# A gated linear attention and feed-forward kernel: TensorE's pads of NOPs placed anew, and the first four total decays turned two heads at a time

## The chip, the cores and the metric

One core of a Trainium2 chip runs the whole program. The metric is the device time of one execution in microseconds (us); the time before is a median of three runs, 522.33 us (521.56 to 523.01).

A core has several engines that run side by side, each with a queue of its own: TensorE (PE; loading the stationary operand is shown apart as PEld), VectorE (DVE), ScalarE (ACT), GpSimd (POOL), and SyncE (SP), which issues the transfers (DMA) here. They wait for each other by semaphores. Each engine has a sequencer that takes the instructions in order and hands them to the engine.

## The reference

Four batches, eight heads, 768 steps, head size 48. In the first half a state of 48 by 48 per head decays by `alpha` and takes in a product of `k` and `v` at each step; the second half is a feed-forward layer with a squared ReLU over 3072 tokens.

```
for t in range(S):
    state = alpha[:, :, t, :, None] * state + np.einsum('bhd,bhe->bhde', k[:, :, t], v[:, :, t])
    y[:, :, t] = np.einsum('bhd,bhde->bhe', q[:, :, t], state)
x = np.ascontiguousarray(y.transpose(0, 2, 1, 3)).reshape(B * S, H * D)
h = np.maximum(x @ w_in, 0.0)
out = (h * h) @ w_out
```

The shapes are `w_in` 384 by 2048 and `w_out` 2048 by 384. Both weights come as 64-bit floats, which the kernel turns into FP32 itself.

## The kernel before, in words

**Tiling.** The 768 steps are cut into six chunks of 128, so there are 24 blocks of 128 tokens (four batches times six chunks), in groups of four blocks (`GB = 4`). For a block, `ln` takes logarithms of alpha, `cs` sums them along the chunk with one product on TensorE, `eb` and `ei` make the running decay `b` and its inverse with exponentials on ScalarE, `mq` and `mk` scale q by `b` and k by the inverse on VectorE, `qT` and `kT` (in later groups `turn`) transpose them on TensorE, `sc`, `kv`, `am` and `us` make scores, state sums, masked scores and sums, `ya` and `yb` give the block's output y, `ev` copies it away, and `st` gives the next state, for which it needs the decay over the whole chunk.

**The total decay.** It is the last row of `b`, needed as a column per head. In the first four blocks TensorE turns it: `lt` (line 345) multiplies, for each of the eight heads, the head's 48 columns of `b` by the last column of the identity matrix; one moving column, a stationary operand of 128 by 48, and the result goes to partitions 0 or 64, by the head's parity. Two copies on ScalarE (line 357) bring it to SBUF. In later blocks a round trip through DRAM does this (`bl`, `br`).

**Stages and order.** The first 33 us are a start in which the first four blocks are prepared; the order of its steps is the list `first` in `AT`, written out by hand, with some products into a bank that nobody reads (`fill`) where TensorE would sit idle. Then six groups follow: each has an input layer and an output layer of the feed-forward part, into which the attention steps of the next group are woven by events with a time in units of work (`weave`). Group 0 works on plain FP32 operands (lines 926 and 816), the later ones on split FP32R operands in three passes (line 733 for the input layer, line 816 for the output layer).

**How products become instructions.** Each pass of a product is a weight load and a matmul. A product of FP32 operands takes two passes, a transpose or an FP32R product one; with this rule the program's products make 5350 matmuls, the number on the page.

**Pads.** Three times the kernel calls `align` (line 1009), at the `turn` of blocks 4, 14 and 16 (`places` in `AT`). `addr_align(256, offset=place)` puts NOPs into TensorE's program until the next instruction stands at place `place` in a block of 256 instructions. The trace has 159 such NOPs: 59, 78 and 22 of them. Counted through the program in this way, the last pads come out at exactly 78 and 22, and the 59 of the first say that 62 places lie ahead of the first instruction counted. So the place of every instruction in its block of 256 is known.

**Waiting.** Most of TensorE's instructions carry their wait with them; where one needs two, a semaphore instruction of the sequencer stands ahead of it, and the sequencer stops there.

Of the kernel before, what the change touches and what calls it, by code (L numbers as in the profile page):

```python
# [12 lines left out]
AF = mybir.ActivationFunctionType  # L13
ALU = mybir.AluOpType
# [1 line left out]


GB = 4
AT = {'v_by': (2.5, 3.5, 5.0), 'before': 2.2, 'places': ((4, 203), (14, 178), (16, 188)), 'evs': 0.65, 'lead': 4, 'post': 3, 'w_first': (45.25, 42.0, 55.95), 'wstep': 1.6, 'w_in_at': 2.5, 'w_in_by': 3.4, 'room1': 22, 'room': 25, 's0': 4, 'ahead': 6, 'late': 2, 'xs': 0.2, 'g0': ((1.5, 4, False, True, 28.25), (20.25, 6, True, True), (28.75, 8, True, False)), 'sc0': (2.35, 2.35, 2.35), 'g1': ((5.5, 8, False, 15.5), (15.5, 10, True), (34.5, 12, True)), 'g': ((1.7, 6, True), (15.5, 8, True)), 'g1x': 50.0, 'gx': 48.25, 'g0x': 55.25, 'k0': 2, 'h0': 16, 'k1': 4, 'h1': 3, 'h1by': 2, 'evs0': 0.3, 'tp': 'ADMD', 'tp1': 'ADAD', 'split': 8, 'o0': (44.75, 47.25), 'o1': (), 'o2': (21.75, 27.5, 31.75, 35.0, 41.25, 41.75), 'str1': 22.0, 'ga': 9.5, 'gb': 13.0, 'cv0': 1.5, 'first': 'ln0 warm0 cs0 load0v load2a ei0 load1v eb0 mk0 ln1 fill1 fill1 kT0 cs1 kc0 eb1 mq0 qT0 mq1 ei1 qc0 fill1 mk1 fill1 lt0 sc0 lt1 kT1 kv0 qT1 am0 ln2 weights2 us0 load2q kc1 qc1 cs2 sc1 fill1 am1 load2k ei2 load3a eb2 load4a fill1 kv1 st0 first0 us1 fill1 middle0 ln3 mq2 load3k ya0 qT2 yb0 mk2 fill1 qc2 kT2 cs3 kc2 load3q load2v weights5 sc2 eb3 load3v fill1 sga0 weights3 sgb0 fill1 ei3 ev0 mq3 mk3 am2 fill1 qT3 kT3 sgc0 first1 kc3 qc3 middle1 kv2 weights4 ha0 sc3 us2 kv3 sga1 ha1 am3 us3 sgb1 load4k ya2 load4q load4v first2 yb2 sgc1 middle2 weights6 lt3 ev2 lt2 st2 ha3 ha2 sgb2 sga2 hb1 sgc2 hb0 hb2 weights1 st1 hb3 st3 weights0'}


RUN = {0: 128, 32: 32, 64: 64, 96: 32}
# [3 lines left out]
def kernel(  # L26
# [12 lines left out]
    nc = tc.nc  # L39
    B, H, S, D = q.shape  # L40
    C = 128
# [39 lines left out]
    def two_k(name, dt=FP32, shape=(GB * C,)):  # L81
        return two_pool.tile([128, *shape], dt, tag="two", name=name)
# [7 lines left out]
    def flat(t):  # L90
        return t.rearrange("a x y -> a (x y)")
# [3 lines left out]
    for x, n in (("q", 2), ("q", 3), ("k", 3)):  # L95
        t = lent[x, n] = two_k("qk_lent", shape=(H, 64))
        nc.gpsimd.memset(t[:, :, D:64], 0.0)

    def tile_of(x, n):
        return lent.get((x, n), tiles[x][n % len(tiles[x])])  # L100
# [127 lines left out]
    ident = consts.tile([128, 128], FP32, name="ident")  # L228
# [9 lines left out]
    for t in s_all + u_all:  # L238
        nc.gpsimd.memset(t, 0.0)
    last = consts.tile([128, 4, NP], FP32, name="last")  # L240
    nc.gpsimd.memset(last, 0.0)
    last_t = [last[:, i, :] for i in range(4)]
    dram = ctx.enter_context(tc.tile_pool(name="dram", bufs=1, space=bass.MemoryType.DRAM))
# [15 lines left out]
    blk = [{} for _ in range(NBLK)]  # L259
# [4 lines left out]
    def bank(n, name, shape=(NP, C)):  # L264

        return ps_att.tile([128, *shape], FP32, tag="att", name=name)
# [10 lines left out]

    SPLIT = AT["split"]

# [22 lines left out]
    def sums_of_logs(n):  # L302
        return blk[n]["cs"].rearrange("a p t -> a (p t)")[:, 0 : H * D]

    def eb(n):
        b = blk[n]["b"] = p2.tile([128, H * D], FP32, tag="b", name="b")
        nc.scalar.activation(out=b, in_=sums_of_logs(n), func=AF.Exp)

# [3 lines left out]

    def scaled(x, n, factor):
        t = tile_of(x, n)[:, :, 0:D]
        nc.vector.tensor_tensor(
            out=t, in0=t, in1=factor.rearrange("a (h d) -> a h d", h=H), op=ALU.mult
        )

    def mq(n):
        need(("q", n))  # L320
        scaled("q", n, blk[n]["b"])
        given.add(("qb", n))

    def mk(n):
        need(("k", n))
        scaled("k", n, blk[n].pop("inv"))
        given.add(("kb", n))
# [17 lines left out]
    def lt(n):  # L345

        ps = bank(n, "lastT")
        for p in range(NP):
            for e in range(2):
                nc.tensor.matmul(  # L350
                    out=ps[64 * e : 64 * e + D, 0, p : p + 1],
                    lhsT=blk[n]["b"][:, (2 * p + e) * D : (2 * p + e + 1) * D],
                    rhs=ident[:, C - 1 : C], start=True, stop=True, skip_group_check=True,
                )
        for e in range(2):
            rows = slice(64 * e, 64 * e + D)
            nc.scalar.copy(out=last_t[n % 4][rows, :], in_=ps[rows, 0, 0:NP])
        given.add(("last", n))
# [290 lines left out]
    here, todo, room = {}, [], [22]  # L649
# [28 lines left out]
    def diff_w(w, p):  # L678
# [5 lines left out]
        for x in "ld":  # L684
            t = made.pop((x, w, p))
            if w == "i" or p >= NW - AT["k0"] or (x == "l" and p >= NW - AT["k1"]):
                here[x, w, p] = t
        pump()

    def prepare(at, w, p):  # L690
        step = AT["wstep"]
        fs = (cast_w, rest_w, scale_w, diff_w)
        return [(at + i * step, f, (w, p)) for i, f in enumerate(fs)]
# [82 lines left out]
    def splits_of_x(at, g):  # L776
        return [(at + i * AT["xs"], f, (g, i % KM)) for i, f in enumerate((split_x,) * KM + (diff_x,) * KM)]

    def layer_in(g):
        units = []  # L780
        for n in range(NJ + 2):
            if n < NJ:
                units.append((1.05, in_x, (n,)))
            if 0 <= n - 2 < NJ:
                units.append((0.53, in_y, (n - 2,)))
            if 0 <= n - AT["post"] < NJ:
                units.append((0, in_post, (n - AT["post"],)))
            if AT["lead"] <= n < AT["lead"] + AHEAD and (g > 1 or AT["k1"] == NW):
                units += splits_of_h(0, n - AT["lead"])
        return units  # L790
# [168 lines left out]


    steps = {f.__name__: f for f in (ln, sp, cs, eb, ei, mq, mk, bl, br, lt, qT, qc, kT, kc, ev)}
    steps["sc"], steps["kv"], steps["am"] = scores, state_sums, masked
    steps["us"], steps["st"] = sums_copied, next_state
# [14 lines left out]
    first = AT["first"]  # L978
# [28 lines left out]
    places = dict(AT["places"])  # L1007
# [51 lines left out]
    def weave(units, events, at):  # L1059
        for cost, f, args in units:  # L1060
            while events and events[0][0] <= at:
                _, e, given = events.pop(0)
                e(*given)
            f(*args)
            at += cost
        for _, e, given in events:
            e(*given)
# [44 lines left out]
    base = [0]  # L1112
    cv0 = AT["cv0"]
    events = [(3.4 * i + cv0, next_weights, (3 + i,)) for i in range(-3, 2 * NW - 3) if ("mid", 3 + i) not in given]
# [11 lines left out]
    for g in range(1, NG):  # L1126
        base.append(begin + sum(u[0] for u in units))
        at0 = base[g]
        units.append((0, begun, (g,)))
        units += layer_in(g) + layer_out(g)  # L1130
        units.append((0, ended, (g,)))
        if g + 1 < NG:
            for t, n0, after, *other in AT["g1"] if g == 1 else AT["g"]:
                n0 = n0 if g == 1 else n0 + GB * g
                other = [None if x is None else at0 + x for x in other]
                events += attention(at0 + t, n0, after, 1, True, *other)
            events += [(at0 + t, f, x) for t, f, x in splits_of_x(AT["g1x" if g == 1 else "gx"], g + 1)]
        if g == 1:
            m = len(AT["w_first"])
            for p in range(m, NW):  # L1140
                events += prepare(at0 + AT["w_in_at"] + AT["w_in_by"] * (p - m), "i", p)
            for i, at in enumerate(AT["o1"] + AT["o2"]):
                events += prepare(at0 + at, "o", order[len(AT["o0"]) + i])
            n = min(AT["k0"], AT["k1"])
            events.append((at0, lambda: todo.extend(("l", "o", p) for p in range(NW - n, NW)), ()))
            events.append((at0 + AT["str1"], stream_out, (AT["k1"], "d")))
        events.append((at0 + 26, stream, (g + 1,)))
    weave(units, sorted(events, key=lambda x: x[0]), begin)


# [28 lines left out]
```

## Time and profile before

| what | before |
|---|---|
| median of 3 runs | 522.33 us |
| the profiled execution's own time | 521.93 us |
| its span, from first to last instruction | 520.1 us |
| granted TensorE clock, mean | 0.999 |
| TensorE busy | 511.3 us, 5350 matmuls |
| VectorE busy | 362.3 us |
| ScalarE busy | 315.6 us |
| HBM traffic over the span | 195 GB/s |
| TensorE busy of the first 33 us | 29.44 us |
| TensorE busy from 33 to 125 us | 92.00 us |
| TensorE busy from 219 to 226 us | 5.32 us of 7 |

The profiled execution's time is 1.83 us more than its span, and 0.40 us under the median of the runs. Times of single instructions below are counted from the start of the span. A line such as `9.74 0.53 PE L350 MATMUL lastT<-ident,b 128*48 128x1 f32 x16` says: from 9.74 us on, for 0.53 us, 16 matmuls of line 350 on TensorE, with a stationary operand of 128 by 48 and one moving column; in brackets at the end stands the idle time before it and what ended it. Matmuls are pipelined: the time from one start to the next, and not the duration, is what one costs. `PEldq` is the sequencer of TensorE's queue.

### The profile page before, as it was taken

How to read it: one execution, taken by the hardware profiler on the slowest of the kernel's cores; microseconds unless marked ns; L12 is line 12 of the kernel's file. 1: busy time of each engine (PE TensorE's matmuls, PEld its weight loads, DVE VectorE, ACT ScalarE, POOL GpSimd, SP SyncE). 2: the span in 40 equal slices, each digit the busy share in tenths (PEclk: the TensorE clock that was granted, in tenths of full speed). 3: DMA queues.
4: the chain of work that ended last, by engine and by line, in shares of the span. 5: the costliest groups of instructions: out<-in, count | busy, mean ns of one | idle time of the engine just before them, and what ended most of it. 6: DMA issues, size and time to landing. Idle time of an engine off the chain costs nothing.

```text
span 520.1 us, 13202 instructions
## 1 busy us (share of the span) xinstructions
PE 511.3 (98%) x5350; PEld 421.9 (81%) x5350; DVE 362.3 (70%) x629; ACT 315.6 (61%) x664; POOL 5.3 (1%) x29
## 2 busy tenths in 40 slices
PE   8999999999999999989999999999999999999997
PEld 6775446668887669968899988899988899988997
DVE  3987979999879579757596466696465485363861
ACT  5678893687999566466953266962266863164620
POOL 4000000000000000000000000000000000000000
PEclk9999999999999999999999999999999999999999
DMA  9999686417888496998885796955683534798201
GB/s 185 214 269 253 180 209 180 67 61 231 242 229 199 121 279 162 309 306 227 183 238 163 245 268 185 227 174 163 214 273 123 182 123 153 252 355 294 70 0 62
DMA packets 139324, 102.36 MB, mean 197 GB/s; under 512 B 109808, under 2 KB 112896, under 8 KB 139264
## 3 DMA queue, kind: packets, MB, share of 16 engines
q1 hardware_dynamic: 139264, 101.52, 68.5%
q8 instruction: 43, 0.70, 0.5%
q14 instruction: 17, 0.14, 0.1%
HBM read 84.17 MB, written 17.33 MB: 195 GB/s over the span
## 4 chain that ended last, share of the span: by engine, by line
PE 92%; DVE 3%; ACT 2%; DMA 1%; issue 1%; SPq 0%; DVEq 0%; POOLq 0%
PE o L816 40%; PE h L733 31%; PE h L926 8%; PE y L409 4%; PE sckv L429 2%; PE T L586 2%; PE sckv L457 2%; DMA a_in<-in_alpha_dram 1%; ACT x L624 1%; PE cs L296 1%; PE cs L299 1%; PE cs L300 1%; DVE x L624 0%; DVE osb L656 0%; DVE xl L656 0%
## 5 line engine op out<-in xcount | busy, mean ns | idle before, releaser
L733 PE MATMUL h<-xa,wb 128*128 128x512 f32 x240 | 69.2, 396 | 0.0
L733 PE MATMUL h<-xd,wd 128*128 128x512 f32 x240 | 66.9, 394 | 1.8 <-ACT ha L706 1.7
L733 PE MATMUL h<-xl,wl 128*128 128x512 f32 x240 | 68.2, 392 | 0.0
L750 ACT ACTIVATE h<-h 128x512 f32<-128x512 f32 x40 | 23.3, 582 | 57.5 <-PE h L733 57.3
L656 DVE TENSOR_TENSOR hid<-h,hid 128x512 f32<-128x512 f32 x40 | 27.5, 688 | 42.7 <-PE h L733 39.9
L624 ACT COPY x<-y 32x256 f32<-32x256 f32 (+2 forms) x132 | 47.1, 364 | 15.2 <-PE y L409 13.0
L816 PE MATMUL o<-wb,ha 128*128 128x384 f32 x160 | 54.2, 339 | 0.0
L733 PEld LDWEIGHTS h<-xd,wd 128*128 128x128 f32 x240 | 44.4, 188 | 11.6 <-ACT ha L706 2.1
L816 PE MATMUL o<-wd,hd 128*128 128x384 f32 x304 | 53.7, 335 | 0.0
L816 PE MATMUL o<-wl,hl 128*128 128x384 f32 x160 | 53.6, 335 | 0.0
L816 PE MATMUL o<-w_out,hid 128*128 128x384 f32 x160 | 53.5, 490 | 0.0
L733 PEld LDWEIGHTS h<-xl,wl 128*128 128x128 f32 x240 | 44.9, 188 | 10.5 <-ACT wl L675 0.6
L816 PEld LDWEIGHTS o<-wd,hd 128*128 128x128 f32 x304 | 52.8, 188 | 0.0
L733 PEld LDWEIGHTS h<-xa,wb 128*128 128x128 f32 x240 | 44.3, 188 | 9.5 <-ACT xa L706 0.3
L816 PE MATMUL o<-wb,hx 128*128 128x384 f32 x144 | 48.8, 339 | 0.0
L816 PE MATMUL o<-wl,hx 128*128 128x384 f32 x144 | 48.2, 335 | 0.0
L816 PEld LDWEIGHTS o<-w_out,hid 128*128 128x128 f32 x160 | 30.0, 190 | 19.6
L926 PE MATMUL h<-x,w_in 128*128 128x512 f32 (+1 forms) x120 | 42.8, 510 | 0.2 <-DVE w_in L206 0.2
L706 ACT ACTIVATE ha<-hid 128x512 fp32r<-128x512 f32 x40 | 25.5, 636 | 23.8 <-DVE hx L656 13.1
L748 ACT ACTIVATE hid<-h 128x512 f32<-128x512 f32 x40 | 24.2, 606 | 25.2 <-PE h L733 25.1
L926 PEld LDWEIGHTS h<-x,w_in 128*128 128x128 f32 x120 | 22.5, 190 | 17.2 <-issue 14.2
L656 DVE TENSOR_TENSOR hl<-hid,ha 128x512 fp32r<-128x512 f32 x40 | 27.5, 686 | 11.2 <-ACT ha L706 11.2
(115 smaller groups left out, 883.7 us busy)
## 6 DMA issues: line engine op xcount, KB each, us to landing
wd<-do SPq DMA_DIRECT2D x36, 384.0 KB
wl<-lo SPq DMA_DIRECT2D x34, 384.0 KB
wl<-li SPq DMA_DIRECT2D x32, 384.0 KB
wd<-di SPq DMA_DIRECT2D x32, 384.0 KB
raw<-in_moe_w_in_dram SPq DMA_DIRECT2D x8, 768.0 KB
raw<-in_moe_w_out_dram SPq DMA_DIRECT2D x8, 768.0 KB
v_in<-in_v_dram SPq DMA_DIRECT2D x24, 192.0 KB
out_dram<-osb SPq DMA_DIRECT2D x24, 192.0 KB
```

The source lines that it names most:

```text
L409: ins = nc.tensor.matmul(out=ys[e][64 * half : 64 * half + D + G * e, m % 2, p // 2, t], lhsT=lhsT, rhs=rhs, start=(half, e) not in seen, ...
L429: nc.tensor.matmul(out=ps[e][HALF[h], 0, p, :], lhsT=ks[rows, p, HALF[h]], rhs=qs[rows, p, HALF[h]], start=True, stop=True, skip_group_che ...
L457: nc.tensor.matmul(out=ps[h][64 * e : 64 * (e + 1), 1, p, G:64], lhsT=tile_of("k", n)[HALF[h], 2 * p + e, :], rhs=tiles["v"][n % NV][HALF[ ...
L586: nc.tensor.transpose(out=ps[h][:, i, p, :], in_=rows[HALF[h], 128 * p : 128 * (p + 1)], identity=ident[HALF[h], HALF[h]],)
L624: copy(out=x[kk][to : to + m, t : t + 2], in_=blk[n]["y"][e][r : r + m, :, p // 2],)
L656: nc.vector.tensor_tensor(out=o, in0=x, in1=z, op=op)
L706: nc.scalar.activation(out=a, in_=x, func=AF.Copy, scale=NEAR)
L733: nc.tensor.matmul(out=acc["h", j], lhsT=here[w, "i", p][:, kk, jj * 128 : (jj + 1) * 128], rhs=x_parts[x][:, kk], start=start and kk == 0 ...
L748: nc.scalar.activation(out=hid[j], in_=x, func=AF.Copy, scale=E)
L750: nc.scalar.activation(out=x, in_=x, func=AF.Copy, scale=1.0 + E)
L816: nc.tensor.matmul(out=acc[t][:, 0:DM], lhsT=lhs[:, t * C : (t + 1) * C], rhs=rhs, start=start, stop=stop, skip_group_check=True,)
L926: nc.tensor.matmul(out=ps, lhsT=w[:, kk, c0 : c0 + 128], rhs=xT[g][kk][:, cols], start=(kk == 0), stop=(kk == KM - 1),)
```

## The change

Two parts of the kernel change.

The decay `b` of the first four blocks gets a tile of its own with each head's 48 columns at a pitch of 64 (`wide`, four tiles; their gaps are zeroed on GpSimd at the start). `eb` writes it with gaps, `mq` reads it so, and `lt` takes two heads at once: a stationary operand of 128 by 128, one moving column, all 128 partitions of the result. That is four products for a block in place of eight, or 8 passes in place of 16.

The pads: the one at the turn of block 14 (78 NOPs) becomes three, of 26 NOPs each, by the new list `pads` of (group, time in the group, place). At the turn of block 4 the place becomes 143, and a further pad follows at time 20 of group 0. Since 64 instructions of TensorE are gone, counting gives 63 NOPs for the former and 60 for the latter; behind these, from place 1572 of the program on, every instruction stands where it stood before, but for the stretch of the three pads.

The entries of `AT` that change (the rest of that line is the same):

```
-'places': ((4, 203), (14, 178), (16, 188))
+'places': ((4, 143), (16, 188)), 'pads': ((0, 20.0, 36), (1, 52.0, 11), (2, 0.5, 83), (2, 5.5, 178))
```

```
+    wide = [two_k("b_wide", shape=(H, 64)) for _ in range(GB)]
...
+    for t in wide:
+        nc.gpsimd.memset(t[:, :, D:64], 0.0)
...
     def eb(n):
+        if n < GB:
+            b = blk[n]["b"] = wide[n]
+            out, in_ = (x.rearrange("a (h d) -> a h d", h=H) for x in (flat(b), sums_of_logs(n)))
+            nc.scalar.activation(out=out[:, :, 0:D], in_=in_, func=AF.Exp)
+            return
...
     def scaled(x, n, factor):
         t = tile_of(x, n)[:, :, 0:D]
-        nc.vector.tensor_tensor(
-            out=t, in0=t, in1=factor.rearrange("a (h d) -> a h d", h=H), op=ALU.mult
-        )
+        if len(factor.shape) == 2:
+            factor = factor.rearrange("a (h d) -> a h d", h=H)
+        nc.vector.tensor_tensor(out=t, in0=t, in1=factor[:, :, 0:D], op=ALU.mult)
...
     def lt(n):
 
         ps = bank(n, "lastT")
+        rows_of_b = flat(blk[n]["b"])
         for p in range(NP):
-            for e in range(2):
-                nc.tensor.matmul(
-                    out=ps[64 * e : 64 * e + D, 0, p : p + 1],
-                    lhsT=blk[n]["b"][:, (2 * p + e) * D : (2 * p + e + 1) * D],
-                    rhs=ident[:, C - 1 : C], start=True, stop=True, skip_group_check=True,
-                )
+            nc.tensor.matmul(
+                out=ps[:, 0, p : p + 1], lhsT=rows_of_b[:, 128 * p : 128 * (p + 1)],
+                rhs=ident[:, C - 1 : C], start=True, stop=True, skip_group_check=True,
+            )
...
+    events += [(base[g] + t, align, (place,)) for g, t, place in AT["pads"]]
     weave(units, sorted(events, key=lambda x: x[0]), begin)
```

More of the change, by code (lines that the diff above doesn't have):

```diff
@@ L18 @@
 GB = 4
-AT = {'v_by': (2.5, 3.5, 5.0), 'before': 2.2, 'places': ((4, 203), (14, 178), (16, 188)), 'evs': 0.65, 'lead': 4, 'post': 3, 'w_first': (45.25, 42.0, 55.95), 'wstep': 1.6, 'w_in_at': 2.5, 'w_in_by': 3.4, 'room1': 22, 'room': 25, 's0': 4, 'ahead': 6, 'late': 2, 'xs': 0.2, 'g0': ((1.5, 4, False, True, 28.25), (20.25, 6, True, True), (28.75, 8, True, False)), 'sc0': (2.35, 2.35, 2.35), 'g1': ((5.5, 8, False, 15.5), (15.5, 10, True), (34.5, 12, True)), 'g': ((1.7, 6, True), (15.5, 8, True)), 'g1x': 50.0, 'gx': 48.25, 'g0x': 55.25, 'k0': 2, 'h0': 16, 'k1': 4, 'h1': 3, 'h1by': 2, 'evs0': 0.3, 'tp': 'ADMD', 'tp1': 'ADAD', 'split': 8, 'o0': (44.75, 47.25), 'o1': (), 'o2': (21.75, 27.5, 31.75, 35.0, 41.25, 41.75), 'str1': 22.0, 'ga': 9.5, 'gb': 13.0, 'cv0': 1.5, 'first': 'ln0 warm0 cs0 load0v load2a ei0 load1v eb0 mk0 ln1 fill1 fill1 kT0 cs1 kc0 eb1 mq0 qT0 mq1 ei1 qc0 fill1 mk1 fill1 lt0 sc0 lt1 kT1 kv0 qT1 am0 ln2 weights2 us0 load2q kc1 qc1 cs2 sc1 fill1 am1 load2k ei2 load3a eb2 load4a fill1 kv1 st0 first0 us1 fill1 middle0 ln3 mq2 load3k ya0 qT2 yb0 mk2 fill1 qc2 kT2 cs3 kc2 load3q load2v weights5 sc2 eb3 load3v fill1 sga0 weights3 sgb0 fill1 ei3 ev0 mq3 mk3 am2 fill1 qT3 kT3 sgc0 first1 kc3 qc3 middle1 kv2 weights4 ha0 sc3 us2 kv3 sga1 ha1 am3 us3 sgb1 load4k ya2 load4q load4v first2 yb2 sgc1 middle2 weights6 lt3 ev2 lt2 st2 ha3 ha2 sgb2 sga2 hb1 sgc2 hb0 hb2 weights1 st1 hb3 st3 weights0'}
@@ new lines @@
+AT = {'v_by': (2.5, 3.5, 5.0), 'before': 2.2, 'places': ((4, 143), (16, 188)), 'pads': ((0, 20.0, 36), (1, 52.0, 11), (2, 0.5, 83), (2, 5.5, 178)), 'evs': 0.65, 'lead': 4, 'post': 3, 'w_first': (45.25, 42.0, 55.95), 'wstep': 1.6, 'w_in_at': 2.5, 'w_in_by': 3.4, 'room1': 22, 'room': 25, 's0': 4, 'ahead': 6, 'late': 2, 'xs': 0.2, 'g0': ((1.5, 4, False, True, 28.25), (20.25, 6, True, True), (28.75, 8, True, False)), 'sc0': (2.35, 2.35, 2.35), 'g1': ((5.5, 8, False, 15.5), (15.5, 10, True), (34.5, 12, True)), 'g': ((1.7, 6, True), (15.5, 8, True)), 'g1x': 50.0, 'gx': 48.25, 'g0x': 55.25, 'k0': 2, 'h0': 16, 'k1': 4, 'h1': 3, 'h1by': 2, 'evs0': 0.3, 'tp': 'ADMD', 'tp1': 'ADAD', 'split': 8, 'o0': (44.75, 47.25), 'o1': (), 'o2': (21.75, 27.5, 31.75, 35.0, 41.25, 41.75), 'str1': 22.0, 'ga': 9.5, 'gb': 13.0, 'cv0': 1.5, 'first': 'ln0 warm0 cs0 load0v load2a ei0 load1v eb0 mk0 ln1 fill1 fill1 kT0 cs1 kc0 eb1 mq0 qT0 mq1 ei1 qc0 fill1 mk1 fill1 lt0 sc0 lt1 kT1 kv0 qT1 am0 ln2 weights2 us0 load2q kc1 qc1 cs2 sc1 fill1 am1 load2k ei2 load3a eb2 load4a fill1 kv1 st0 first0 us1 fill1 middle0 ln3 mq2 load3k ya0 qT2 yb0 mk2 fill1 qc2 kT2 cs3 kc2 load3q load2v weights5 sc2 eb3 load3v fill1 sga0 weights3 sgb0 fill1 ei3 ev0 mq3 mk3 am2 fill1 qT3 kT3 sgc0 first1 kc3 qc3 middle1 kv2 weights4 ha0 sc3 us2 kv3 sga1 ha1 am3 us3 sgb1 load4k ya2 load4q load4v first2 yb2 sgc1 middle2 weights6 lt3 ev2 lt2 st2 ha3 ha2 sgb2 sga2 hb1 sgc2 hb0 hb2 weights1 st1 hb3 st3 weights0'}
```

## The prediction

> **What bounds the kernel now.** I read the page first, then TensorE's time line around each edited place, then the chain of waits in the start.
>
> ```profile
> PE 511.3 (98%) x5350; PEld 421.9 (81%) x5350; DVE 362.3 (70%) x629; ACT 315.6 (61%) x664; POOL 5.3 (1%) x29
> q8 instruction: 43, 0.70, 0.5%
> PE 92%; DVE 3%; ACT 2%; DMA 1%; issue 1%; SPq 0%; DVEq 0%; POOLq 0%
> ```
>
> TensorE is busy for 511.3 of 520.1 us and 92% of the chain, so what it gains or loses moves the end. The second line matters below: 43 packets of 16 KB carry the program to TensorE, one for each block of 256 instructions.
>
> The time line of TensorE at the long pad, and the pad's NOPs in that stretch:
>
> ```profile
> L1011 PEldq NOP  x78: 13/13/13, 219.6 to 225.2; - x78
> 222.81 0.86 PE L733 MATMUL h<-xl,wl 128*128 128x512 f32 x3
> 225.35 0.94 PE L733 MATMUL h<-xd,wd 128*128 128x512 f32 x3 [1.68 <-ACT ha L706]
> ```
>
> The NOPs follow each other every 0.0725 us (5.6 us by 77), five times what their record says. The sequencer runs ahead: setting the program's order beside the trace's starts, 33 loads and matmuls are still to start when the first NOP runs, and at nearly all of its stops. That is 16.5 passes of 0.227 us, 3.7 us of cover for 5.6 us. The last of the three earlier matmuls starts at 223.27, the next at 225.35: 2.08 in place of 0.23. The page names ScalarE, which had long been done; it is the pad.
>
> The turning of two decays, and what a load costs:
>
> ```profile
> 7.60 0.30 PEld L296 LDWEIGHTS cs<-a_in,causal 128*128 128x128 f32 x2 [0.41 <-ACT a_in L274]
> 9.74 0.53 PE L350 MATMUL lastT<-ident,b 128*48 128x1 f32 x16
> 10.20 0.70 PE L429 MATMUL sckv<-qs,ks 48*64 48x64 f32 x32
> ```
>
> The 16 passes of 48 columns start every 0.0225 us. Two loads of 128 columns, 0.19 us each, take 0.30 together: the second starts 0.108 after the first.
>
> The chain of waits in the start (start, us, what):
>
> ```profile
> 9.81 0.46 PE lastT L350 x16
> 10.27 0.62 PE sckv L429 x32
> ...
> 14.58 0.76 DVE am L440 x2
> ...
> 25.37 1.53 PE h L926 x6
> ...
> 29.74 0.75 issue
> 30.49 0.52 PE y L409 x20
> ...
> 32.36 0.82 PE lastT L350 x32
> ```
>
> All four turnings lie on it. VectorE's chain from 14.58 to 25.2 is without a gap and begins when the scores of block 1 are there, behind two turnings. At 29.74 TensorE waits for nothing that the profile shows. By the count of places, the matmul at 30.49 is the first instruction of block 4 of the program.
>
> **The change part by part**, against the profiled execution's 521.93 us.
>
> *The long pad in three: -1.93 us.* The stall of 1.84 goes, and 0.09 more, which the first load after it cost (its three passes take 0.78, not 0.69). Each new pad is 26 x 0.0725 = 1.89 us. The first stands in output passes of 0.174 us, with 33 ahead: 2.9 us of cover. The second comes behind a wait for a transfer, which ended at 213.25 with 19 ahead; the passes up to the pad end at 215.7, the NOPs at some 215.2: 0.45 us to spare. The third has 3.7 us. Without this cover each costs up to 1.9. Between the pads the sequencer makes up its lead in 0.7 us (37 instructions, near 35 us). What is later earlier by 1.9 us are the weight tiles read back; from 265 us on nearly every stop of the sequencer has 33 ahead, so transfers do not hold it, and I keep the whole gain. Bounds -2.0 and -1.2.
>
> *The turnings: +1.73 us.* No row has a load of 128 columns with one moving column. From below, transposes load 128 columns every 0.06; from above, the FP32 loads 0.108. I take 0.108: that row has this type and width, and a matmul of one column is too short to hide it. Then 8 x 0.108 = 0.86 against 16 x 0.0225 = 0.36, +0.50 for each of four. A change of operand shape costs 0.09 (last fill to first turning 0.31, not 0.215); with full width one such change falls away at the first, the second and the last turning: -0.27. So +1.73, of which +0.82 in the first two, and +0.1 with the lower price. Nothing hides it: VectorE's gapless chain starts that much later.
>
> [...]
>
> *The pads of group 0: +1.35 us.* The first has 63 NOPs for 59, 4.6 us under 33 passes and loads of 0.43 us a pass (7.1 us): nothing. The second, 60 NOPs or 4.35 us, follows the transposes of block 5 by only six passes of `h`:
>
> ```profile
> 61.19 0.42 PE L586 MATMUL T<-ident,q_in 64*128 64x64 f32 x8
> 61.54 10.57 PE L926 MATMUL h<-x,w_in 128*128 128x512 f32 x24
> ```
>
> With 33 ahead at most, 12 of them the six passes, the first NOP cannot run before the 21st last of 64 transposing instructions starts, at 61.04. The last ends at 65.39. The six passes are through at 61.54 + 0.53 + 5 x 0.43 = 64.22. The next starts at some 65.47: 1.25, and 0.1 for the first load. TensorE is busy in every microsecond from 33 to 125 us, so nothing later takes it back. Bounds 0 (a deeper queue than the 33 seen) and 1.6.
>
> *The wait for block 4: from 0.96 to some 1.6, +0.64.* In the trace the packet that starts at 27.89 lands at 28.98, and block 4's first matmul starts 1.51 later, where 0.96 was lost. That packet is due when the sequencer nears block 3, at some 21.7, so it lay 6.2 us behind other transfers; the next, due at 27.7, started at 31.62, 3.9 late. With 32 instructions gone, block 3 begins among the products behind `kT3`, where the sequencer stops for VectorE until 23.7 (trace of before), with the two turnings 24.5. Midway between 6.2 and 3.9 the packet starts at 29.6, and block 4 is ready at 29.6 + 1.1 + 1.5 = 32.2. Its first instruction, 32 places further on, would start at 30.76 - 0.96 + 0.82 = 30.6. Lost: 1.6. Bounds 0 (lateness under 3.5) and 3.
>
> *At nothing:* four memsets on GpSimd (some 0.64 us by their neighbours, done at 6.8, first needed at 9.7); `eb` and `mq` with a pitch of 64 keep their element counts, and `mq` reads and writes such a pitch already; no wait is added on ScalarE, VectorE or SP, and their order stays. If pitch made `eb` dearer, it would count twice in the start.
>
> Sum: -1.93 + 1.73 + 1.35 + 0.64 = +1.79, so 523.72 by the profiled execution. That lay 0.40 under the median of the runs, so I forecast **524.1 us**.
>
> **The rivals.**
> 1. *The block arrives in time* (ends on the other side: not slower). If the packet waits for a fixed backlog rather than a fixed time, it still starts near 27.9, and at 30.5 nothing is lost: 1.6 less, 522.5. It decides as soon as the lateness is under 3.5 us. For it: later in the run most packets start within 3 us of being due. Against: all five in the first 40 us were late by 2.7 to 6.4. [...]
> 2. *Wide loads at the transposes' price*: 1.6 less, 522.5. For it, matmuls of one column leave the array free; against, the 0.108.
> 3. *The start takes the delay up*: if conversion of the weights on VectorE, not TensorE, sets the first 75 us, then the turnings, the pad of group 0 and the wait for block 4 change nothing, and 3.72 fall away: 520.4. For it: the sequencer's stop at 64.3 waits for VectorE. Against: 21 instructions lay ahead then, 4.6 us.
> 4. *The three pads find a shorter queue*, because transfers come later against TensorE: the 1.93 come back, 526.0. For it: two of the pads stand next to waits for transfers, one with 0.45 to spare.
>
> **How the numbers follow.** Forecast 0.41, rivals 0.19, 0.14, 0.19, 0.07. A measurement here can tell 0.3% (1.57 us) from no change, so slower begins at 523.9. Slower: forecast and rival 4, 0.48, less 0.04 for forecasts that fall just short: 0.44. Same: rivals 1 and 2 and those 0.04, 0.37. Faster (520.8 and less): rival 3, 0.19. The range: a lateness from 0 to 6.4 us moves the forecast from 522.5 to 525.4; rival 4 above is taken in, and half of rival 3 below: 520.4 to 526.0. The forecast's own, with one unknown at a time at its bounds, is 522.5 to 525.5.
>
> **What would show it.** Long pad: no idle time of TensorE near 222 to 226 and none longer than 0.2 at the three pads. Turnings: the eight passes start some 0.108 apart, the first turning to the scores is 0.4 us longer. Group 0: idle time of some 1.25 on line 935 near 64 to 66. Block 4: an "issue" wait near 31 in the products of line 418, its length by the third instruction packet. The forecast is wrong if the first turnings start no later than 0.06 apart, if TensorE does not idle near 65, or if the time up to the first group is no longer than before.

## The result, and the profile after

In the first comparison the changed kernel took 526.67 us (median of 8 runs, 525.41 to 527.87) where the kernel before took 522.77: ratio 1.0069, 95% interval 1.0047 to 1.0091, 2.5 to 4.8 us slower. The profiled execution took 525.91 us (span 523.8), 3.98 more than that of before. The direction was forecast; the forecast itself, 524.1, and its range up to 526.0 lay too low. Of the 2.55 us between 524.12 and 526.67, 0.44 are the kernel before itself, whose three runs ahead of the forecast had a median of 522.33.

The page of the changed kernel: its TensorE line, the granted clock in 40 slices, and the chain by engine.

```profile
PE 515.3 (98%) x5318; PEld 424.6 (81%) x5318; DVE 362.1 (69%) x629; ACT 316.2 (60%) x664; POOL 5.9 (1%) x33
...
PEclk9989999999999999999999999999999999999999
...
PE 87%; DVE 5%; ACT 4%; SPq 1%; DMA 1%; issue 1%; DVEq 0%; POOLq 0%
```

TensorE is busy 4.0 us longer with 32 matmuls fewer, so part of the loss hides in matmuls that last longer. The 8 in the third slice (26 to 39 us) says where: the clock was not granted in full. The page of before has a 9 there. Its windows, cut at the borders of the slow stretch (start and end in us; then busy us and instructions of TensorE, its loads, VectorE, ScalarE and GpSimd; granted clock; share of the DMA engines; GB/s):

```profile
31.49:34.90 3.41, 3.23 (x88) 3.02 (x89) 2.74 (x6) 2.26 (x5) 0.00 (x0) 1.00 0.94 234
34.90:38.31 3.41, 3.41 (x10) 2.78 (x10) 2.38 (x6) 2.55 (x10) 0.00 (x0) 0.50 0.81 292
38.31:41.70 3.39, 3.39 (x17) 2.98 (x17) 3.29 (x8) 2.01 (x5) 0.00 (x0) 1.00 0.23 50
```

For 3.41 us (34.90 to 38.31) TensorE was granted 0.50 of its clock: 10 matmuls where the next stretch has 17. In the kernel before, TensorE was about as busy in the window at this place (3.28 and 3.23 us), and the next one ran at full clock:

```profile
31.34:34.75 3.41, 3.28 (x86) 2.89 (x75) 2.60 (x7) 2.58 (x8) 0.00 (x0) 1.00 0.66 103
34.75:38.16 3.41, 3.41 (x17) 3.02 (x16) 2.92 (x6) 3.22 (x10) 0.00 (x0) 1.00 0.93 332
```

In the changed kernel's time line of that place, behind the first turning's line:

```profile
9.80 0.95 PE L360 MATMUL lastT<-ident,b_wide 128*128 128x1 f32 x8
...
33.11 1.97 PE L360 MATMUL lastT<-ident,b_wide 128*128 128x1 f32 x16
34.94 3.85 PE L935 MATMUL h<-x,w_in 128*128 128x256 f32 x9
```

Eight wide passes take 0.95 us (sixteen narrow ones took 0.53); two turnings together hold the array for 1.9 us, and right behind them the clock is halved. The passes of `h` start 0.427 apart there and 0.216 apart from 38.4 on, as they did throughout before.

The second pad of group 0, in the time line:

```profile
65.01 2.84 PE L935 MATMUL h<-x,w_in 128*128 128x512 f32 x6
68.97 3.24 PE L935 MATMUL h<-x,w_in 128*128 128x512 f32 x7 [1.11 <-ACT qs L603]
```

Six passes, 1.11 us of idle time as the view counts it (it names ScalarE, as it did at the long pad), then the next. From start to start it is 1.71 in place of 0.43. The first short pad, in the time line of TensorE, then VectorE's line there and the pad's NOPs:

```profile
213.84 2.94 PE L825 MATMUL o<-wd,hd 128*128 128x384 f32 x16
217.04 3.04 PE L825 MATMUL o<-wd,hd 128*128 128x384 f32 x16 [0.26 <-issue]
```

```profile
213.00 1.95 DVE L862 SCALAR_TENSOR_TENSOR osb<-o,osb 128x384 f32<-128x384 f32 x4
```

```profile
L1020 PEldq NOP  x26: 13/13/13, 215.0 to 217.0; - x26
```

The NOPs begin at 215.01, 0.06 after VectorE's fourth operation ended (214.95), and end at some 217.0; the next output pass starts then, at 217.04, 0.60 after the one ahead of it in place of 0.17. At the third short pad, where the long one stood, nothing idles any more:

```profile
226.80 0.86 PE L742 MATMUL h<-xd,wd 128*128 128x512 f32 x3
227.50 0.85 PE L742 MATMUL h<-xa,wb 128*128 128x512 f32 x3
228.19 0.85 PE L742 MATMUL h<-xl,wl 128*128 128x512 f32 x3
228.88 0.84 PE L742 MATMUL h<-xd,wd 128*128 128x512 f32 x3
```

Matching every matmul of the two traces in the program's order, the changed kernel's delay grows in these steps (us):

| step | forecast | profiled runs |
|---|---|---|
| first two turnings | +0.82 | +0.87 |
| last two turnings | +0.91 | +1.04 |
| wait for block 4 (0.96 before, 0.86 after) | +0.64 | -0.08 |
| half clock, 34.90 to 38.31 | none | +1.51 |
| second pad of group 0 | +1.35 | +1.41 |
| first short pad | 0 | +0.52 |
| long pad gone | -1.93 | -1.74 |
| drift later, and outside the span | 0 | +0.45 |
| sum | +1.79 | +3.98 |

### The profile page after: what moved, and what is told of

The parts are those of the page before. It is cut to its first block, busy times and chain, and to the rows that moved or that the text cites. A ratio compares the mean times of both kernels' runs of the same rounds, so it can differ in the third digit from the quotient of the medians.

```text
span 523.8 us, 13206 instructions
## 1 busy us (share of the span) xinstructions
PE 515.3 (98%) x5318; PEld 424.6 (81%) x5318; DVE 362.1 (69%) x629; ACT 316.2 (60%) x664; POOL 5.9 (1%) x33
## 4 chain that ended last, share of the span: by engine, by line
PE 87%; DVE 5%; ACT 4%; SPq 1%; DMA 1%; issue 1%; DVEq 0%; POOLq 0%
PE o L825 40%; PE h L742 30%; PE h L935 4%; PE y L418 4%; PE sckv L438 2%; PE T L595 2%; PE sckv L466 2%; SPq L353 1%; DMA a_in<-in_alpha_dram 1%; ACT x L633 1%; DVE w_in L200 1%; PE lastT L360 1%; ACT power L180 1%; PE cs L305 1%; PE cs L301 1%
## 5 line engine op out<-in xcount | busy, mean ns | idle before, releaser
L935 PE MATMUL h<-x,w_in 128*128 128x512 f32 (+1 forms) x120 | 44.7, 527 | 1.4 <-ACT qs L603 1.1
L935 PEld LDWEIGHTS h<-x,w_in 128*128 128x128 f32 x120 | 23.6, 200 | 19.1 <-issue 14.2
```

The lines of the kernel that those rows point to most:

```text
L935: nc.tensor.matmul(out=ps, lhsT=w[:, kk, c0 : c0 + 128], rhs=xT[g][kk][:, cols], start=(kk == 0), stop=(kk == KM - 1),)
```

## The experiments

Each kernel was timed against the kernel before on its own chip; ratios are to that, and a difference between two kernels' medians is from two comparisons. In the first expectations theory A is the right column of the table. Kernels with narrow turnings are the changed kernel with the old `eb` and `lt`; the four memsets on GpSimd stay in them. A run whose mean granted clock is 0.997 or less is counted as one with a halved window: 3.41 us at 0.50, as in the changed kernel's trace, take 0.0033 off the mean over its 523.8 us.

**Turnings narrow, all pads kept.** `lt` again as before (two products a pair, 16 passes), `eb` and `b` too, and the first pad's place 144 in place of 143, so that all that follows keeps its place:

```
-AT 'places': ((4, 143), (16, 188))
+AT 'places': ((4, 144), (16, 188))
...
+                for e in range(2):
+                    nc.tensor.matmul(
+                        out=ps[64 * e : 64 * e + D, 0, p : p + 1],
+                        lhsT=blk[n]["b"][:, (2 * p + e) * D : (2 * p + e + 1) * D],
...
```

> The changed kernel with its four pads in group 0 and the long stretch, but the four turnings made one head at a time again (16 narrow passes each). The pads keep every later instruction in its place: the second pad of group 0 has 59 NOPs, the first none. Theory A (from the two traces): the wide turnings cost 1.9 us of spacing, and by leaving one free-running window of 3.4 us with almost nothing streaming they also halve TensorE's clock for the next window, 1.5 us more in the profiled run. Both go: 526.7 - 1.9 - 1.5 or more = 523.3 or less, granted clock 0.998 or more in nearly every run. Rival B: the half-speed window is a chance of the launch and not the turnings' doing: 526.7 - 1.9 = 524.8, and clocks from 0.993 to 1.000 as in the changed kernel's runs. Rival C (the forecast's own count): turnings 1.73 and the wait for block 4 0.64: 524.3, clocks without pattern.

Measured: 522.60 us, ratio 0.9998 (0.9989 to 1.0008), 1 of 11 runs with a halved window. Theory A holds; B's 524.8 and C's 524.3 do not. The turnings and what they do to the clock are the whole loss; the pads, taken together, come out even, to within 0.5 us by the interval.

**The three short pads alone.**

```
-AT 'places': ((4, 203), (14, 178), (16, 188))
+AT 'places': ((4, 203), (16, 188)), 'pads': ((1, 52.0, 11), (2, 0.5, 83), (2, 5.5, 178))
```

> The kernel before with nothing changed but its long pad parted into three. Theory A: the long pad's stall of 1.84 us and 0.09 for the cold load go; the first short pad stalls TensorE by 0.42 us and 0.09, because its sequencer stood at a wait for VectorE eight instructions earlier and had only 17 loads and matmuls ahead: 1.3 to 1.4 us less than before, 521.4. Rival (the forecast's count): the sequencer keeps 33 ahead at the first pad, which is free: 1.93 less, 520.8, and no idle time of TensorE near the first pad. Rival: the gain is lost later to transfers: 522.8 as before.

Measured: 521.22 us, ratio 0.9970 (0.9957 to 0.9983), 0.9 to 2.3 us faster. The interval holds both 1.4 and 1.9; the trace decides between them: 0.60 from pass to pass at the first short pad, as in the changed kernel, 17 loads and matmuls ahead.

**The second pad of group 0 later.**

```
-'pads': ((0, 20.0, 36),
+'pads': ((0, 24.0, 60),
```

> The changed kernel with the second pad of group 0 (60 NOPs) moved 24 instructions later, so that 18 passes of h lie between the transposes and the pad instead of 6. Theory A: the pad's stall of 1.28 us and 0.13 for the cold load go, and nothing else changes: 526.7 - 1.4 = 525.3, no idle time of TensorE near 64 to 70 us. Rival (the start takes delays up, the pace of the first 75 us being set by VectorE's conversions): TensorE waits for weights in place of the pad, 526.7 as it was.

Measured: 525.42 us, ratio 1.0040 (1.0019 to 1.0060), and in its time line the passes run through:

```profile
65.41 0.42 PE L595 MATMUL T<-ident,q_in 64*128 64x64 f32 x8
65.76 10.57 PE L935 MATMUL h<-x,w_in 128*128 128x512 f32 x24
```

24 passes take the 10.57 us that they took before. The pad stops nothing; the medians differ by 1.25 us (526.67 and 525.42), near the 1.41 of the table, though the intervals of the two ratios overlap. The start does not take the pad's stall up: rival 3 of the prediction falls. 8 of its 10 runs still had a halved window.

**One long pad in the changed kernel.**

```
-'places': ((4, 143), (16, 188)), 'pads': ((0, 20.0, 36), (1, 52.0, 11), (2, 0.5, 83), (2, 5.5, 178))
+'places': ((4, 143), (14, 178), (16, 188)), 'pads': ((0, 20.0, 36),)
```

> The changed kernel with the three short pads made one long pad of 78 NOPs again, where it stood before. Theory A: 1.84 us of stall and 0.09 for the cold load come back, 0.51 for the first short pad goes: 526.7 + 1.4 = 528.1. Rival (all three short pads are free): 526.7 + 1.93 = 528.6. Rival (the pads never decided anything): 526.7.

Measured: 527.06 us, ratio 1.0087 (1.0069 to 1.0106). Beside the changed kernel's 1.0069 that is too little to tell 1.4 us from nothing; the runs with the pads alone settle the gain, this one does not. In its trace the long pad's 2.08 us is back, and where the first short pad had stood the output passes wait 0.43 us for a tile read back. Its profile caught two halved windows in a row:

```profile
30.97:34.38 3.41, 2.86 (x85) 2.66 (x85) 2.90 (x6) 2.31 (x5) 0.00 (x0) 1.00 0.74 140
34.38:37.80 3.42, 3.42 (x11) 2.89 (x11) 2.37 (x7) 2.50 (x8) 0.00 (x0) 0.50 1.02 359
37.80:41.20 3.40, 3.40 (x9) 2.70 (x8) 3.30 (x7) 1.36 (x4) 0.00 (x0) 0.50 0.36 85
```

**More columns past the same loads.** Is it the wide loads, the time, or how little streams? A wide turning streams the last 64 columns of the identity in place of one:

```
-                out=ps[:, 0, p : p + 1], lhsT=rows_of_b[:, 128 * p : 128 * (p + 1)],
-                rhs=ident[:, C - 1 : C], start=True, stop=True, skip_group_check=True,
+                out=ps[:, p, 0:64], lhsT=rows_of_b[:, 128 * p : 128 * (p + 1)],
+                rhs=ident[:, C - 64 : C], start=True, stop=True, skip_group_check=True,
...
-            nc.scalar.copy(out=last_t[n % 4][rows, :], in_=ps[rows, 0, 0:NP])
+            nc.scalar.copy(out=last_t[n % 4][rows, :], in_=ps[rows, 0:NP, 63])
```

> The changed kernel with one thing altered: each wide turning streams the last 64 columns of the identity past its loaded rows instead of the last one (the copies take the last of the 64). The products keep their loads, count and places; only more columns stream. Theory A: TensorE's clock is halved for a window of 3.4 us when, in the window before it, the columns streamed (each weighted by the part of the array that its tile takes) are under about a fifth of what full speed allows. Counted from the traces, the windows ahead of the three halved ones had 0.14, 0.17 and 0.14; the lowest window that was followed by full speed had 0.24. Turnings 2 and 3 now stream 1024 columns more, an eighth of a window's 8192, 0.27 in all: clock 0.998 or more in nearly every run, and 526.7 - 1.5 to 2.0 = 524.9 or less, spacing of the passes still 0.112. Rival B: the clock goes by the time TensorE waits or by its instructions, or by chance: clocks of 0.992 to 0.997 in most runs as in the changed kernel (7 of 8 there), 526.7. Rival D: 64 columns make each pass longer (0.16 in place of 0.112): slower than 526.7 though the clock stays up.

Measured: 524.35 us, ratio 1.0016 (1.0006 to 1.0026), clock 0.999 or 1.000 in all 10 runs. Time line and windows:

```profile
33.01 2.00 PE L360 MATMUL lastT<-ident,b_wide 128*128 128x64 f32 x16
34.84 5.40 PE L935 MATMUL h<-x,w_in 128*128 128x256 f32 x24
```

```profile
31.55:34.95 3.40, 3.27 (x89) 3.07 (x90) 2.99 (x7) 2.47 (x6) 0.00 (x0) 1.00 0.84 168
34.95:38.40 3.45, 3.45 (x18) 3.04 (x18) 2.40 (x6) 3.23 (x11) 0.00 (x0) 1.00 1.00 335
```

The turnings last as long as with one column (2.00 and 1.97, the passes 0.112 apart in both), TensorE is as busy in the window ahead (3.27 and 3.23), and yet the clock stays whole: 24 passes of `h` take 5.40 us, where 16 took 5.36 in the changed kernel. More work made the kernel 2.3 us faster, by the medians. Rivals B and D fall.

**Which turnings.** In `eb` and `lt`, the condition for the wide form is `n in (0, 1)`, and in the other kernel `n in (2, 3)`.

> The changed kernel with turnings 2 and 3 (those behind the wait for block 4, just ahead of group 0) made one head at a time again; 0 and 1 stay wide. Everything behind stays in its place. Theory A: the low window ahead of group 0 comes from turnings 2 and 3 (1.83 us with hardly a column): clock 0.998 or more in nearly every run, and 1.0 us of spacing less as well: 526.7 - 1.0 - 1.5 to 2.0 = 523.9. Rival B: clock without pattern, 525.7.

> The changed kernel with turnings 0 and 1 made one head at a time again; 2 and 3 stay wide. Theory A: the low window stays, so most runs show 0.992 to 0.997; 0.8 us of spacing goes: 526.7 - 0.8 = 525.9. Rival B: clock without pattern. Rival E (the start makes up for the first turnings, since the later wait for block 4 ends at the same time): 526.7.

Measured: 523.25 us, ratio 1.0010 (0.9996 to 1.0023), 3 of 12 runs halved, with 0 and 1 wide; 526.14 us, ratio 1.0050 (1.0034 to 1.0067), 5 of 6 halved, with 2 and 3 wide. It is, for most halved runs, the pair ahead of group 0. Rival E and theory A (526.7 and 525.9) cannot be told apart by 526.14. The three halved runs of the first were not expected, and made the next step: the windows have no fixed place against the start (their borders stand at 34.90 us in the trace of the changed kernel, 34.86 with 2 columns, 34.75 in before and 34.38 with one long pad), and of one kernel's runs only a share is halved, 3 of 12 here. No trace caught one of these three; by the count below, this kernel's low windows begin near 10 us, at the first pair.

**Fewer columns.** The same edit with 24, 2 and 8 columns.

> As the run with 64 columns, but each wide turning streams the last 24 columns of the identity. Theory A in numbers: slide a window of 3.413 us over the traces in forty steps and ask how often some window of the start holds less than 0.19 to 0.20 of the columns of full speed (weighted by tile). That gives a share of runs with a halved window for each kernel so far: changed kernel 0.93 (7 of 8 seen), later pad of group 0 0.93 to 0.98 (8 of 10), long pad 0.90 to 0.95 (5 of 6), wide 2 and 3 0.73 to 0.75 (5 of 6), wide 0 and 1 0.28 to 0.30 (3 of 12), before 0.15 to 0.18 (2 of 22 and 7 of 27), narrow 0 (1 of 11), 64 columns 0 (0 of 10). With 24 columns put into the same traces it is 0.20 to 0.35 (by the trace with 64) to 0.60 to 0.73 (by that of the changed kernel): about half of the runs at 0.993 to 0.997, the others at 0.999 or 1.000, and the two groups 1.5 us or more apart; median 525.4. Rival (any second column wakes the gate): clock 0.999 or more in all, 524.4. Rival (only a full stream does): as the changed kernel, 526.7.

> As the run with 24 columns, but each wide turning streams the last 2 columns of the identity, into four places of the bank as the runs with 24 and 64 columns do. Open after 0 halved runs of 12 with 24 columns: whether the gate counts columns, with a limit nearer 0.18 than 0.20 of full speed, or whether any second column (or the other place of the result) keeps the clock up. Theory A: 2 columns change the lowest window by 0.002 only: half to all of the runs at 0.992 to 0.997 (0.65 to 0.85 of them by a limit of 0.18 put into the traces), median 525.5 to 526.7. Rival F (any second column, or the other place): clock 0.999 or more in all, 524.3.

> The same with the last 8 columns. Theory A (columns counted, limit near 0.18): 0.50 to 0.78 of the runs with a halved window, fewer than with 1 or 2 columns, more than with 24 (0 of 12). Rival F: none.

Measured: 24 columns 524.25 us, ratio 1.0025 (1.0012 to 1.0038), 0 of 12 halved, where about half were expected: the limit of 0.19 to 0.20 was too high. 2 columns 527.69 us, 1.0086 (1.0065 to 1.0106), 6 of 6 halved, which ends rival F; the median is 1 us above the forecast for it, as four of the six lost two windows. 8 columns 524.77 us, 1.0054 (1.0035 to 1.0073), 3 of 6. What is counted: each matmul's columns, times the part of the array that its tile takes, in a window of 3.413 us (the length of the slow stretch in the changed kernel's trace), divided by the 8,192 that the expectation with 64 columns gives a window. No trace shows 8,192 columns in a window, so it is a divisor and no more: plain FP32 passes, all that the start has, stream 256 columns in 0.215 us, some 4,060 in a window, and 0.18, some 1,475 columns, is 0.36 of that.

The table puts a limit of 0.18 into each kernel's own trace, in which a halved window is first set back to full speed. The first share is of forty even positions of the window, the second of the positions that the window had in the fourteen traces; nine of those lie within half a microsecond of each other.

| kernel | even positions under 0.18 | the traces' positions under 0.18 | runs halved |
|---|---|---|---|
| changed, 1 column | 0.70 | 0.93 | 7 of 8 |
| 2 columns | 0.78 | 0.93 | 6 of 6 |
| 8 columns | 0.53 | 0.93 | 3 of 6 |
| 24 columns | 0.08 | 0.07 | 0 of 12 |
| 64 columns | 0 | 0 | 0 of 10 |
| wide 2 and 3 | 0.45 | 0.86 | 5 of 6 |
| wide 0 and 1 | 0.18 | 0 | 3 of 12 |
| narrow, all pads | 0 | 0 | 1 of 11 |
| before | 0.08 | 0 | 11 of 83 |

By the even positions the order of the kernels comes out, the shares only roughly (by the others 8 columns should have been halved in nearly every run): the wait for block 4 (0.42 to 1.39 us in the profiles) moves the turnings from run to run, and one trace stands for each kernel. The limit was fitted after 24 columns; 2 and 8 columns were forecast with it.

**The first short pad earlier, and two pads in place of three**, both in the kernel before:

```
+'pads': ((1, 48.0, 218), (2, 0.5, 83), (2, 5.5, 178))
...
+'pads': ((2, 0.5, 70), (2, 5.5, 178))
```

> The kernel before with its long pad in three, as in the run with the pads alone, but the first short pad 49 instructions earlier: ahead of the waits of the output passes for VectorE, not eight instructions behind the last of them. Theory A (a wait carried by a pass holds the sequencer as long as it lasts, so a pad in front of it runs within that wait): the 0.42 and 0.09 of the first short pad go, 521.2 - 0.5 = 520.7, no idle time of TensorE near 211 to 213 us. Rival (a pad costs what is not ahead of it in the queue, wherever it stands): 521.2 as with the pads alone. It would be the fastest of all.

> The kernel before with its long pad of 78 NOPs in two of 39, both in products of h at the places where the changed kernel has its second and third short pad. Theory A: 39 x 0.0725 = 2.83 us each; 29 loads and matmuls were ahead at the first place and 33 at the second, of 0.227 us a pass: 3.3 and 3.7 us of cover. Neither stalls TensorE: the whole 1.93 go, 0.5 less than with three pads (0.3% below the kernel before there): ratio 0.996, some 520.9 where the kernel before takes 522.8. Rival (fewer, longer pads stall again): idle time of TensorE at one of the two, ratio 0.998 or more.

Measured: 521.60 us, ratio 0.9970 (0.9959 to 0.9981), and 521.65 us, 0.9972 (0.9957 to 0.9986). Both expectations were half wrong. The earlier pad met 24 loads and matmuls ahead and stalled for 0.19 us, not 0; the first of the two pads met 21, not 29, and stalled for 0.48:

```profile
215.62 0.85 PE L752 MATMUL h<-xl,wl 128*128 128x512 f32 x3
216.78 0.47 PE L752 MATMUL h<-xa,wb 128*128 128x512 f32 x1 [0.31 <-PE h L752]
```

The three versions cannot be told apart by their times. All beat the kernel before by 0.3% and the changed one by about 1%: of the change, the parted pad is worth keeping.

## Why the prediction was wrong

**The missing term: the clock.** The sum took every pass at the duration that before shows. No step and no rival asked whether TensorE keeps its clock, since the page of before shows 9 in every slice. The wide turnings put 1.9 us with hardly a column next to the wait for block 4 and the narrow products, and most runs (7 of 8 in the first comparison) then lose half the clock for one or two windows: 1.51 us in the profiled run, 2.3 between the medians with 1 and 64 columns. This alone takes 524.1 out of reach. Before's trace held a warning: by the same count its lowest window ranges from 0.18 to 0.29 of the scale with the window's position, and two turnings twice as long can only lower it. The limit itself could not be read there.

**"The first stands in output passes of 0.174 us, with 33 ahead: 2.9 us of cover."** It had 17 ahead and 1.6 us (215.01 to 216.62), and the pad took 2.0, not 1.89. The 33 were counted at stops that wait for transfers or for the queue. The passes ahead of this pad each carry a wait for VectorE, and the sequencer stood there until VectorE was done: in all ten traces that have this pad at this place, its first NOP comes 0.06 us after VectorE's fourth operation. In eight of them one NOP is 0.225 us behind the one ahead of it, and the stall is 0.39 to 0.43; in the two without this gap (later pad of group 0, 2 columns) it is 0.27. What makes the gap was not traced. In before, VectorE's fourth operation ended at 210.11, 1.66 us ahead of the pass where the pad went in (211.77): a stall of some 0.3 for 1.89 us of NOPs could have been read. The second and third short pads were free here, as forecast; with 24 columns, the third met 25 ahead and stalled for 0.7.

**The wait for block 4, +0.64: not there.** The third packet started at 28.99, not 29.6, and block 4 ran 1.35 after it landed, not 1.5; TensorE arrived at about the forecast time (30.68), so 0.86 was lost where 1.6 was forecast. The profiles after it show 0.42 to 1.24 us in kernels with narrow turnings of 0 and 1 and 0.57 to 1.39 in those with wide ones: the wait scatters more from run to run than the change moves it. Rival 1 had nothing lost, a step of -0.96; the step of -0.08 lies between it and the forecast, and the block did not arrive in time.

**The turnings, +1.73: right in kind, 0.18 too small.** The passes start 0.112 apart, not 0.108, 0.13 us over 32 passes. Rival 2, the transposes' price, falls.

**The pad of group 0, +1.35, and the long pad, -1.93: right**, at 1.41 and -1.74, and the run with the pad moved shows that nothing later takes it back. At the former 38 loads and matmuls were ahead, more than the 33 that the prediction set as the most; the NOPs took 4.48 us in place of 4.35, and the two errors nearly cancel. Rival 4 came true in part: one pad of three found a shorter queue, by waits for VectorE and not by transfers.

**What stays open.** With the clock whole (64 and 24 columns) the kernel is 0.16 and 0.25% slower than before, 0.8 and 1.3 us, where the terms without the clock add up to 2.0. Before's own halved runs explain some 0.2 of that (11 of 83, about 1.6 us each). The terms also rest on a quick execution of before: its 521.93 us is 0.84 under the median of the first comparison, and of 83 later runs one was quicker; against it, the profiled executions with 64 and 24 columns are 2.8 and 3.2 us longer. What made it quick was not traced.

## What to carry to other kernels

An edit that leaves TensorE busy but streams few columns (here 16 passes of a single column in 1.9 us) can cost clock in the work behind it, 1.51 us in the profiled run: add up the time in which columns stream in every stretch of 3.41 us, at all positions, not busy time (3.23 us of the stretch ahead of the slow one), and look at the granted clock of every run. A cover of queued passes was as long as what the sequencer had ahead at that place (17 loads and matmuls at the first short pad, 33 at the long one), so look for the last wait that a pass ahead carries before putting NOPs there. When a slowdown sits where the edit is not, compare the durations of unchanged instructions first (the passes of `h`, 0.427 and 0.216 us apart).

## What the runs showed of the hardware

These are counts in the traces of this case's fourteen kernels, and they reach no further. In each trace all changes of the granted clock lie a whole number of stretches of 3.413 us apart: in the changed kernel they stand at 4.18, 34.90, 38.31 and 523.01 us, 9, 1 and 142 stretches, and in before at 4.03 and 519.44, 151. Busy time did not tell the stretches apart: the window ahead of the halved one was busy for 3.23 of 3.41 us by the records, with 88 matmuls in it, and the one at this place in before, which full speed followed, for 3.28, with 86. How much streamed, weighted by tile, did: in the start, windows with 0.14 to 0.18 by the count above were followed by half speed, windows with 0.20 or more were not.

Columns alone did not tell them apart, though. At the end of the kernel only FP32R passes stream, 384 columns in 0.173 us, and there windows with 0.25 (one long pad) and 0.27 (8 columns) by that count were followed by half speed too. Put as time (0.84 ns for a column of plain FP32, from 256 in 0.216 us; 0.45 for one of FP32R, from 384 in 0.173; times the part of the array), all windows of the fourteen traces agree: those with columns streaming for at most 0.35 of the window (0.29 in the changed kernel's, at 31.49) were followed by half speed, those with 0.40 or more were not.

The windows at half speed fit this too: those that streamed as much as full speed does in 0.34, 0.38 and 0.39 of a window were followed by another halved one, those with 0.48 and more (0.50 in the changed kernel's, at 34.90) by full speed. Two windows in a row were lost in some runs (clock 0.992 to 0.994): the first slow window began late in the turnings and itself streamed no more than that 0.39, in 11 matmuls with one long pad (34.38 to 37.80) and 12 with 2 columns (34.86 to 38.28).
